# K weights on a second DMA queue, later weights behind the transposes, and a clamp on VectorE: a fused attention and feed-forward kernel

## The chip, the cores and the metric

The kernel runs on one core of one Trainium2 chip. The metric is the device time of one execution in microseconds (us). An execution's time is about 1.7 us more than the span that its profile shows. Medians are quoted with the number of runs. A ratio is the mean time of one kernel's fast runs over that of the other's of the same rounds, so it is not quite the ratio of the medians beside it; its 95% interval stands in brackets. In lines of a profile PE is TensorE, PEld its weight loads, DVE VectorE, ACT ScalarE, POOL GpSimd and SP SyncE; a q behind a name is that engine's instruction queue, L249 a line of kernel.py, and xnT<-xn what an instruction writes and reads.

## The reference

```python
x  = A_x                                   # 1 x 2048 x 576, bf16
xn = layernorm(x)
# A: linear attention, 32 heads of 18
q, k, v = split(xn @ wqkv)                 # 576 x 1728
phi = lambda t: where(t > 0, t + 1, exp(t)) + 1e-6
kv  = sum_s phi(k) v ;  z = sum_s phi(k)
a   = (phi(q) @ kv) / (phi(q) . z + 1e-6) @ wo
# B: gated feed-forward, width 4608
b   = (gelu(xn @ w_gate) * (xn @ w_up)) @ w_down
out = x + a + b
```

## The kernel before: the parts that matter

The order of instructions on each engine is written by hand: every step has a planned time, and the steps are issued sorted by it. Each engine works through its own list in order. A step with a planned time that the chip doesn't keep delays what stands behind it on that engine.

The loads at the start all go through SyncE's queue:

```python
    load_x(0, 1)
    load_x(1, 1)
    load_x(2, 2)
    load_w(1)        # K weights: 576 KB + 72 KB, rows of 1152 bytes
    load_x(4, 2)     # two tiles, rows of 2304 bytes
    load_x(6, 2)
    load_w(0)        # Q weights
    load_x(8, 4)
    load_x(12, 4)
```

For each of 16 tiles of 128 tokens: statistics and norm (VectorE, ScalarE), a transpose (tiles 0 to 3 by TensorE and a copy out of PSUM, tiles 4 to 15 by a crossbar DMA on SyncE's queue), two halves of K (five matmuls each), and the sums G = xn^T phi(K). Twenty Q units run in between and behind. phi is made of four steps per Q unit:

```python
    def q_relu(i): nc.scalar.activation(out=e, in_=ps, func=ACT.Relu, scale=-1.0)        # cut: the tiles
    def q_exp(i):  nc.scalar.activation(out=e, in_=e, func=ACT.Exp, scale=-1.0)
    def q_eps(i):  nc.gpsimd.tensor_scalar(out=e, in0=e, scalar1=1.0, scalar2=EPS_ATT, op0=ALU.mult, op1=ALU.add)
    def q_sum(i):  nc.vector.scalar_tensor_tensor(out=out_, in0=ps, scalar=0.0, in1=e, op0=ALU.max, op1=ALU.add)
```

V's weights and the first gate and up blocks are put between the crossbar transposes, one load each 2.94 us:

```python
    loads = [lambda n, i=i: load_gu(i // 2, i % 2) for i in range(2 * NWBUF)]
    loads.insert(1, lambda n: load_w(2, 0, 2))
    loads.insert(3, lambda n: load_w(2, 2, 4))
    todo += [(18.0 + TILE * i, step, 0) for i, step in enumerate(loads)]
```

Spins (`spin(count)`, matmuls of an identity matrix whose result nobody reads) keep TensorE busy before the first real work.

## Time and profile before

| | before |
|---|---|
| time, median of 4 runs | 525.38 us (524.8 to 525.77) |
| span of the profiled execution (526.45 us, above every timed run) | 524.7 us |
| TensorE busy | 517.2 us, 99% |
| first K matmul; K's main weights landed | 8.24; 8.20 us |
| first gate matmul of the feed-forward | 73.62 us |

TensorE sets the end. Behind 82 us it works without a hole worth naming, so a change to the first part can only move the moment at which the feed-forward starts.

### The profile page before, as it was taken

What the parts mean: (1) busy time and instruction counts of PE and PEld (TensorE: products, weight loads), DVE (VectorE), ACT (ScalarE), POOL (GpSimd) and SP (SyncE); (2) the same over time, 40 slices, a digit from 0 to 9 for tenths busy, and PEclk for the clock granted to TensorE, in tenths of its full rate; (3) what the DMA queues carried; (4) which work ended last, traced back from release to release, by engine and by line L of the source; (5) the groups of instructions that cost most, each with busy time, mean ns of one, the idle gap of its engine ahead of it and who ended that gap; (6) DMA issues with size and microseconds to landing.
All of it is one profiled execution on the core that took longest, in us unless ns stands there. A gap on an engine that the chain in (4) does not pass through costs nothing.

```text
span 524.7 us, 10664 instructions
## 1 busy us (share of the span) xinstructions
PE 517.2 (99%) x4502; PEld 315.8 (60%) x4502; DVE 248.4 (47%) x426; ACT 147.9 (28%) x301; POOL 40.1 (8%) x63
## 2 busy tenths in 40 slices
PE   7999999999999999999999999999999999999997
PEld 7767764555577754444577744444777544445775
DVE  7887545977348423333388134333584233333110
ACT  5989563233230012332200033232000123222000
POOL 2012130121001100000011000000011000000000
PEclk9999999999999999999999999999999999999999
DMA  8565009999500035555300065555100355540000
GB/s 262 135 156 119 1 2 240 264 268 265 169 21 24 12 103 158 158 144 158 108 12 13 28 174 143 156 159 151 32 22 12 104 158 157 144 130 1 12 11 24
DMA packets 106443, 57.90 MB, mean 110 GB/s; under 512 B 13402, under 2 KB 105754, under 8 KB 106394
## 3 DMA queue, kind: packets, MB, share of 16 engines
q1 hardware_dynamic: 106394, 57.21, 38.8%
q8 instruction: 35, 0.57, 0.4%
q14 instruction: 14, 0.11, 0.1%
HBM read 52.86 MB, written 2.36 MB: 105 GB/s over the span
## 4 chain that ended last, share of the span: by engine, by line
PE 96%; DMA 2%; ACT 1%; DVE 0%; SPq 0%; issue 0%; DVEq 0%
PE ps_all L318 55%; PE ps_all L664 27%; PE ps_all L669 4%; PE ps_all L294 3%; PE ps_all L250 3%; PE ps_all L347 3%; DMA wqkv_sb<-in_A_wqkv_dram 1%; DMA xnT<-xn 1%; PE ps_all L442 1%; PE ps_all L424 0%; PE ps_all L646 0%; SPq L93 0%; ACT phi_e L270 0%; DVE hT L278 0%; ACT xnT L239 0%; ACT phi_e L274 0%
## 5 line engine op out<-in xcount | busy, mean ns | idle before, releaser
L318 PE MATMUL ps_all<-xnT,wg 64*128 64x512 bf16 x1152 | 273.0, 376 | 0.0
L318 PE MATMUL ps_all<-xnT,wu 64*128 64x512 bf16 x1152 | 271.6, 376 | 0.0
L635 DVE TENSOR_TENSOR hT<-ps_all,gl 128x512 bf16<-128x512 f32 x144 | 99.4, 691 | 161.2 <-ACT gl L634 160.7
L634 ACT ACTIVATE gl<-ps_all 128x512 f32<-128x512 f32 x144 | 86.0, 598 | 312.7 <-PE ps_all L318 295.8
L318 PEld LDWEIGHTS <-wu 64*128 64x128 bf16 x1152 | 108.1, 94 | 66.0 <-SPq L327 0.7
L318 PEld LDWEIGHTS <-wg 64*128 64x128 bf16 x1152 | 108.1, 94 | 65.7 <-issue 0.5
L664 PE MATMUL ps_all<-wd_sb,hT 128*128 128x288 bf16 x1152 | 147.0, 286 | 0.0
L664 PEld LDWEIGHTS <-hT 128*128 128x128 bf16 x1152 | 112.3, 98 | 30.6 <-issue 1.3
L466 DVE RECIPROCAL den_sb<-den_sb 126x128 f32<-126x128 f32 (+1 forms) x80 | 68.3, 911 | 0.5
L672 DVE TENSOR_TENSOR res<-ps_all,x_sb 128x288 bf16<-128x288 f32 x32 | 14.6, 458 | 88.0 <-PE ps_all L669 88.0
L318 PE MATMUL ps_all<-xnT,wr 64*128 64x512 bf16 x288 | 55.7, 376 | 0.0
L469 POOL TENSOR_TENSOR pqT<-pqT,den_sb 126x512 bf16<-126x512 bf16 (+3 forms) x25 | 24.1, 965 | 299.2 <-DVE den_sb L466 276.0
L669 PE MATMUL ps_all<-m_sb,pqT 126*128 126x288 bf16 (+1 forms) x160 | 24.9, 285 | 0.0
L318 PEld LDWEIGHTS <-wr 64*128 64x128 bf16 x288 | 14.6, 94 | 16.7 <-issue 0.7
L250 PE MATMUL ps_all<-wqkv_sb,xnT 128*128 128x288 bf16 x160 | 22.5, 286 | 1.7 <-DMA wqkv_sb<-in_A_wqkv_dram 0.8
L294 PE MATMUL ps_all<-hT,xn 128*128 128x288 bf16 (+4 forms) x176 | 22.4, 276 | 0.0
L294 PEld LDWEIGHTS <-xn 128*128 128x128 bf16 (+1 forms) x176 | 17.5, 102 | 4.3
L250 PEld LDWEIGHTS <-xnT 128*128 128x128 bf16 x160 | 15.3, 98 | 7.6 <-issue 1.3
L393 DVE SCALAR_TENSOR_TENSOR pqT<-ps_all,phi_e 126x512 bf16<-126x512 f32 (+1 forms) x20 | 13.4, 672 | 12.4 <-POOL phi_e L389 12.4
L669 PEld LDWEIGHTS <-pqT 126*128 126x128 bf16 (+1 forms) x160 | 15.5, 97 | 4.1
L347 PE MATMUL ps_all<-xnT,wqkv_sb 128*126 128x512 bf16 (+1 forms) x70 | 17.4, 378 | 0.0
L389 POOL TENSOR_SCALAR phi_e<-phi_e 126x512 f32<-126x512 f32 (+1 forms) x20 | 12.4, 618 | 54.2 <-DVE hT L278 29.8
(63 smaller groups left out, 183.8 us busy)
## 6 DMA issues: line engine op xcount, KB each, us to landing
wg<-in_B_w_gate_dram SPq DMA_DIRECT2D x72, 256.0 KB, 2.9
wu<-in_B_w_up_dram SPq DMA_DIRECT2D x72, 256.0 KB, 3.5
wd_sb<-in_B_w_down_dram SPq DMA_DIRECT2D x12, 432.0 KB, 4.7
wr<-in_B_w_gate_dram SPq DMA_DIRECT2D x72, 32.0 KB, 2.7
wr<-in_B_w_up_dram SPq DMA_DIRECT2D x72, 32.0 KB, 3.1
out_dram<-res SPq DMA_DIRECT2D x15, 144.0 KB, 1.8
wqkv_sb<-in_A_wqkv_dram SPq DMA_DIRECT2D x2, 576.0 KB, 6.0
x_sb<-in_A_x_dram SPq DMA_DIRECT2D x2, 576.0 KB, 7.2
```

The costliest lines, as they stand in the source:

```text
L250: nc.tensor.matmul(ps_all[:, k_bank(n, hf), :HALF], lhsT=xnT[:, kt, n * P:(n + 1) * P], rhs=wqkv_sb[:, kt, D + hf * HALF:D + (hf + 1) * HALF],
L294: nc.tensor.matmul(ps_all[:m, b, col:col + w], lhsT=xn[:, n, j0:j0 + m], rhs=pk[:, n, d0:d0 + w], start=(n == 0 and col == 0), stop=(n == ...
L318: return nc.tensor.matmul(self.outs[i], lhsT=self.lhs(i, rows, kt), rhs=self.rhs(i, rows, kt), start=start, stop=stop, skip_group_check=True,)
L347: nc.tensor.matmul(ps, lhsT=wqkv_sb[:, kt, q0:q0 + rows], rhs=xnT[:, kt, sc * SC:(sc + 1) * SC], start=(kt == 0), stop=(kt == KT - 1),)
L393: nc.vector.scalar_tensor_tensor(out=out_, in0=ps, scalar=0.0, in1=e, op0=ALU.max, op1=ALU.add)
L466: nc.vector.reciprocal(out=d[:, h:h + P], in_=d[:, h:h + P])
L469: nc.gpsimd.tensor_tensor(out=pqT[:rows, c, cols], in0=pqT[:rows, c, cols], in1=d, op=ALU.mult)
L634: nc.scalar.activation(out=gl[:], in_=ps_all[:, b[0], :], func=ACT.Gelu_apprx_tanh)
L635: nc.vector.tensor_tensor(out=hT[:, GUB * k + i, :], in0=ps_all[:, b[1], :], in1=gl[:], op=ALU.mult)
L664: nc.tensor.matmul(acc, lhsT=hT[:, f, j * P:(j + 1) * P], rhs=wd_sb[:, f, hs], start=(f == 0), stop=False,)
L669: nc.tensor.matmul(acc, lhsT=pqT[:rows, c, ts_], rhs=m_sb[:rows, c, hs], start=False, stop=(c == NCH - 1),)
L672: nc.vector.tensor_tensor(out=res[:, hs], in0=acc, in1=x_sb[:, n, hs], op=ALU.add)
```

## The change

The intent: ScalarE issues the K weights on its own queue, so that they needn't stand behind x tiles in SyncE's; a memset of two elements of the K weights, which the load must wait for, holds it back until the first x tiles are under way. V, gate and up weights no longer mix with the crossbar transposes. The last 8 Q units take exp straight from PSUM and clamp it on VectorE, which spares ScalarE one pass and GpSimd all of its part. A relay (an empty instruction on another engine, which tells TensorE that one half of a block has been written) moves from SyncE to GpSimd for feed-forward block 1. The planned times of nearly all steps change with it. The diff, cut to its core:

```diff
+    def load_w(which, on=nc.sync): ...                       # cut: as before, but in whole, on queue `on`
+    nc.scalar.preload_act_table_set("natural_log_exp_and_others")
     load_x(0, 1)
     load_x(1, 1)
     load_x(2, 2)
-    load_w(1)
-    load_x(4, 2)
-    load_x(6, 2)
+    load_x(4, 4)                                              # rows of 4608 bytes
     load_w(0)
     load_x(8, 4)
     load_x(12, 4)
+
+    nc.vector.memset(wqkv_sb[HP:P, 4, :], 0.0)
+    nc.vector.memset(wqkv_sb[0:1, 0, D:D + 2], 0.0)
+    load_w(1, nc.scalar)
 ...
+    def q_exp1(i): nc.scalar.activation(out=e, in_=ps, func=ACT.Exp)
+    def q_min(i):  nc.vector.tensor_scalar(out=e, in0=e, scalar1=1.0, scalar2=EPS_ATT, op0=ALU.min, op1=ALU.add)
+    def q_max(i):  nc.vector.scalar_tensor_tensor(out=out_, in0=ps, scalar=1.0 + EPS_ATT, in1=e, op0=ALU.add, op1=ALU.max)
 ...                                                           # cut: new planned times of all steps
-    todo += [(t, spin, count) for t, count in [(5.70, 4), (6.23, 3), (6.60, 5), (10.42, 2)]]
+    todo += [(t, spin, count) for t, count in [(5.80, 3), (6.20, 5), (8.50, 2)]]
-    ...                                                       # cut: the loads between the transposes
+    load_w(2)                                                 # behind the last transpose
+    for i in range(NWBUF):
+        load_gu(i, 0)
+        load_gu(i, 1)
-    for step in (q_relu, q_exp, q_eps, q_sum):                # units 12 to 19, three places
+    for step in (q_exp1, q_min, q_max):
-                      nc.sync if blk < 2 else nc.gpsimd)      # relay of a feed-forward block
+                      nc.sync if blk == 0 else nc.gpsimd)
```

## The prediction

> **What bounds the kernel now.** I read the page's busy line and its chain first, to see which engine sets the end.
>
> ```profile
> PE 517.2 (99%) x4502; PEld 315.8 (60%) x4502; DVE 248.4 (47%) x426; ACT 147.9 (28%) x301; POOL 40.1 (8%) x63
> ...
> PE 96%; DMA 2%; ACT 1%; DVE 0%; SPq 0%; issue 0%; DVEq 0%
> ```
>
> TensorE is busy 517.2 of 524.7 us and is 96% of the chain, so only 7.5 us are free at all, and the change removes no real matmul (it drops 4 spin matmuls). The feed-forward part is untouched: three of its four blocks show one unbroken piece of 648 matmuls of 70.03 to 70.04 us in the chain of waits. What can move is the attention head of the program, up to about 82 us. So I listed TensorE's waits in the first 80 us, and then the chain in order of time around each.
>
> ```profile
> PE ps_all L138 <- POOL ident masks.py:199: 1.4, 1, 1.4
> PE ps_all L250 <- DMA wqkv_sb<-in_A_wqkv_dram: 0.8, 1, 0.8
> PE ps_all L250 <- DMA xnT<-xn: 0.7, 1, 0.7
> PE ps_all L236 <- ACT xnT L239: 0.6, 1, 0.6
> PE ps_all L250 <- DVE hT L278: 0.2, 1, 0.2
> ```
>
> ```profile
> 2.20 6.00 DMA wqkv_sb<-in_A_wqkv_dram
> ...
> 8.24 1.40 PE ps_all L250 x10
> ...
> 11.12 0.59 ACT xnT L239
> ...
> 11.75 0.44 PE ps_all L236 x5
> ...
> 15.33 0.83 DVE hT L278 x2
> ...
> 16.20 0.77 PE ps_all L250 x5
> ...
> 25.84 4.52 DMA xnT<-xn
> ...
> 30.41 1.40 PE ps_all L250 x10
> ```
>
> The reader is to see: the first K matmul waits for the K weights, issued at 2.20 and landed 6.00 us later at 8.20. Then there are three holes, before 11.75 (a copy of transposes out of PSUM), 16.20 (a K sum) and 30.41 (a crossbar transpose that took 4.52 us, while others of these transposes took 2.6 to 3.0 us). Together they are 0.6 + 0.2 + 0.7 = 1.5 us. From 30.41 to the feed-forward the chain is TensorE alone.
>
> In the weight-load waits of the stretch 60 to 100 us there is one more, a relay on the sync queue:
>
> ```profile
> PEld L318 <- SPq L327: 0.7, 2, 0.5
> ```
>
> At 80.74 a matmul starts 0.39 us after the one before instead of 0.22, so about 0.2 us of that reaches TensorE.
>
> **What the Trainium skill says.** (1) "DMA: Bandwidth & Descriptors", section "Issuing engines are not separate DMA queues": transfers issued from different engines run on the same 16 DMA engines and interleave; a second issuer saves issue time only. Section "Queues, rings and completion order" of that page adds that each engine round-robins between the queues by packet. The kernel before uses one queue only (page part 3 has all data in q1), so its trace can neither confirm nor deny the sharing. It does show the limit: from 4 to 12 us the DMA share is 0.99 and 1.08 at 313 and 325 GB/s, saturated. (2) "ScalarE: Activation LUTs", section "What ACT_TABLE_LOAD costs": 1283 ns a load; the trace has 1283 ns exactly (0.80 to 2.08 us). (3) "VectorE: DVE Perf Modes", section "The perf-mode tier table (the rule you actually need)": an fp32 tensor_scalar from SBUF runs at 2x, a PSUM operand does not. The trace has no such instruction on VectorE; from PSUM, the 126x512 one takes 0.68 us.
>
> **The change, part by part.**
>
> *K weights on ScalarE's queue.* The issue moves from SyncE at 2.20 us to ScalarE, behind the table load (ends 2.08) and the two memsets on VectorE (the first 0.78 us, from about 0.9: ends near 1.7). So it is issued at about 2.1 to 2.2, no earlier. What changes is the company. Before: first-in first-out behind x tiles 0 to 3 (576 KB), then K (648 KB), and K landed at 8.20. Now x tiles 4 to 7 (576 KB in one transfer with 4608-byte rows instead of two with 2304) are issued on SyncE at about 2.2 and share with K. If K really gets half the engines from about 3.3 us on, with some 350 KB landed by then (117 GB/s over 4 us is 470 KB), it is done when about 350 + 2 x 650 = 1650 KB have moved; at 313 GB/s after 4 us that is about 7.8 us. Larger rows could be quicker per byte: in the kernel before, the two late x transfers of 576 KB landed about 1.4 us apart, against 2.2 us for 576 KB of 1152-byte weight rows. That puts it near 7.3. I take 7.5 for the first K matmul, 0.7 us earlier. Of this 0.3 us goes back, as five transposes (1.40/5 apiece is no guide; 0.28 us between the start of five and what follows at 10.07) now stand behind the first K matmuls instead of ahead of them: net 0.4 us.
>
> *Order of the head.* The instruction orders show K halves, transposes, G sums and Q units reshuffled, with the same work. ScalarE is the tight engine here (3.91 of 4 us busy from 12 to 16, 3.5 to 3.6 to 24). The two holes before 11.75 and 16.20 (0.8 us) are of the old order. I expect new ones in their place, because ScalarE's queue still has copies of transposes between relu and exp: a copy takes 0.69 us, relu 0.41, exp 0.44. Working through the new order by these durations I find three waits of 0.3 to 0.4 us up to the first G sum; but with the second Q unit pulled ahead of the K halves of tile 4, less idle later. Net gain: 0.3 us.
>
> *Later weights behind the transposes.* V and 4 blocks of gate and up weights no longer lie between the 12 transposes. The 4.52 us transpose should be 2.6 to 3.0, and the 0.7 us hole before 30.41 goes. V and the blocks are 18 issues of about 0.45 to 0.6 us, starting near 48: all are issued by about 59 and landed by 62. V is first read at 66.0, block 0 at 73.4. Hidden. Gain: 0.7 us.
>
> *Clamp on VectorE for the last 8 units.* It removes 8 relus (0.60 us, ScalarE) and 8 GpSimd adds (0.62), and adds 8 VectorE min/adds of an estimated 0.33 us (512 elements at 2 per cycle at the page's 0.96 GHz, plus about 60 cycles by the same page). ScalarE's end part, 70.86 to 77.00 before,
>
> ```profile
> 70.86 1.08 ACT L381 ACTIVATE phi_e<-ps_all 126x512 f32<-126x512 f32 x2 [3.64 <-PE ps_all L318]
> ...
> 77.00 1.28 ACT L634 ACT_TABLE_LOAD   x1
> 78.29 1.09 ACT L634 ACTIVATE gl<-ps_all 128x512 f32<-128x512 f32 x2
> ```
>
> shrinks by 6 x about 0.55 = 3.3 us at most; then the first pair of matmul results at about 76.5, not ScalarE, is what the first GELU waits for. But TensorE shows no wait for ScalarE or VectorE there, so of this nothing reaches the end. The relay of feed-forward block 1 moves to GpSimd, which is now idle there: 0.2 us.
>
> Sum: 0.4 + 0.3 + 0.7 + 0.2 = 1.6 us; 525.3 - 1.6 = 523.7 us, which I round down to 523.6 as the two dropped spin groups add a little.
>
> **Rivals.** (a) *K comes no earlier*, or later: if the engines alternate by row and not by bytes, a 4608-byte x row is moved for each 1152-byte K row, and K waits until x tiles 4 to 7 are through, past 8.2 us. For it: the DMA is saturated, and nothing is taken out ahead of K. Against it: K's rows need not queue behind x tiles 2 and 3 any more. Also, x tiles 2 and 3 (landed near 5.4) could come later, and their statistics stand ahead of the copy of tile 0's last transposes on VectorE. Time then about 525. (b) *ScalarE takes over.* From 12 to 48 us it is 85 to 98% busy; a TensorE that starts earlier may just catch it up and wait, so that only part of the gain stays: about 524.5. Against it: TensorE was never seen to wait for it after 12 us. (c) *Everything fits*: K at 7.0, no new holes, 1.2 + 1.5 + 0.2 = 2.9 us: 522.4. (d) *Late weights stall the feed-forward*: would need 11 us of delay; I give it almost nothing.
>
> **Range and chances.** 523.6 us, from 522.3 (rival c) to 525.2 (rival a). Faster by over 2% would need 514.8, more than all 7.5 us of TensorE's idle time; slower by over 2% would need a new stall of 10.5 us, and none is in sight. Within 2%: 0.98.
>
> **What would show it.** First K matmul at 7.3 to 7.8 and K's landing beside it; ScalarE's queue as a second data queue. No transpose above about 3.2 us, and no TensorE wait for one. Table load for GELU near 74 to 75 instead of 77.0. The feed-forward's three unbroken 70.0 us pieces unchanged. TensorE's waits in the first 80 us (without the first, for the identity) down from 2.3 us to about 1. Wrong if K lands after 8.2, if x tiles 2 and 3 land after 6, or if new waits on ScalarE's or VectorE's copies exceed 1.5 us.

## The result, and the profile after

The changed kernel took 526.88 us (median of 4, 526.42 to 527.52) against 525.38: ratio 1.003 [1.0013, 1.0048]. It is about 1.5 us slower, where about 1.7 us less were predicted. It is within 2%, but outside the range and on the wrong side.

The page's busy line and chain of the changed kernel look almost as before:

```profile
PE 517.4 (99%) x4498; PEld 314.8 (60%) x4498; DVE 250.9 (48%) x435; ACT 143.2 (27%) x293; POOL 35.2 (7%) x55
```

"TensorE busy" is no help here: a matmul at half clock counts as busy too. TensorE's waits in the first 80 us, the same view as before (us in total, times, longest):

```profile
PE ps_all L249 <- DMA wqkv_sb<-in_A_wqkv_dram: 3.1, 1, 3.1
PE ps_all L137 <- POOL ident masks.py:199: 1.4, 1, 1.4
PE ps_all L249 <- DMA xnT<-xn: 0.2, 1, 0.2
```

The waits for ScalarE's copy and for VectorE's K sum are gone, as meant, but the wait for K's weights grew from 0.8 to 3.1 us. The chain in order of time (start, duration, what):

```profile
0.80 1.15 ACT L114
1.95 7.64 DMA wqkv_sb<-in_A_wqkv_dram
9.59 0.04 issue
9.63 1.36 PE ps_all L249 x5
10.99 0.53 PE ps_all L235 x5
11.52 1.20 PE ps_all L249 x5
```

K was issued at 1.95, 0.25 us earlier than before, and landed 1.39 us later. The earlier issue won nothing: the first row of K moved at 4.02 us, and at 4.01 in the kernel before. The five K matmuls at 11.52 then took 1.20 us; ten of them took 1.40 us before. Why the rate halved is in the table of stretches (length, busy time of TensorE, its weight loads, VectorE, ScalarE and GpSimd, then the granted TensorE clock, DMA share, GB/s):

```profile
8.00:10.00 2.00, 0.37 (x2) 0.26 (x2) 0.41 (x2) 0.00 (x0) 0.24 (x1) 0.80 1.12 303
10.00:12.00 2.00, 2.00 (x13) 1.45 (x11) 0.00 (x0) 0.85 (x2) 0.00 (x0) 0.50 1.03 315
12.00:14.00 2.00, 2.00 (x20) 1.59 (x18) 1.37 (x4) 1.97 (x7) 0.24 (x1) 0.85 0.69 279
```

After 3.1 us without work the clock was granted at half until some way past 12 us. All four runs have a mean clock of 0.996 or 0.997; the kernel before has 0.999 or 1.000. The Trainium skill ("TensorE: Matmul & The Clock Gate", section "What's actually happening") says that a window of about 3.4 us without work halves the clock and another one of work restores it; the trace agrees in kind: half lasted 3.4 us, from 9.20 to 12.62. But the gap that did it was only 3.1 us long, and in the run b3_no_hold below one of 2.0 us was followed by 3.4 us of half clock as well (9.28 to 12.70), so here less than a whole window without work was enough.

What the DMA engines did, by queue (packets, MB, share of 16 engines; q1 is SyncE's, q10 ScalarE's with nothing but K on it). Between 3 and 4 us, though K had been issued at 1.95, q10 moved nothing:

```profile
q1 hardware_dynamic: 86, 0.16, 97.2%
```

Between 4 and 6 us:

```profile
q1 hardware_dynamic: 171, 0.58, 73.8%
q10 hardware_dynamic: 174, 0.20, 29.5%
```

And between 7 and 8 us, when x tiles 4 to 7 were nearly through and the Q weights followed them:

```profile
q10 hardware_dynamic: 177, 0.20, 55.4%
q1 hardware_dynamic: 163, 0.19, 53.4%
```

In these two stretches the queues moved about as many packets each (nearly all of them rows): 174 of K to 171 of the other. But most x rows of the first stretch were 4608 bytes long and a K row 1152, so K got 0.20 of 0.78 MB. When the Q rows came, as short as K's, K got half and no more, and from 8 to 9 us only 97 of 292 packets. Before, all of this stood behind K in one queue. That the engines take turns row for row is no rule, though: two runs below (a2_x_small_rows, b5_only_k_queue) gave K clearly more than half of the rows.

Later in the chain, the slow crossbar transpose that the change was to remove:

```profile
45.96 4.34 DMA xnT<-xn
50.35 1.40 PE ps_all L249 x10
```

No weight load is beside it any more (the first is issued at 50.22), and still it took 4.34 us. ScalarE's end part, as shown of before:

```profile
72.47 1.09 ACT L398 ACTIVATE phi_e<-ps_all 126x512 f32<-126x512 f32 x2 [4.31 <-PE ps_all L317]
74.41 2.05 ACT L398 ACTIVATE phi_e<-ps_all 126x512 f32<-126x512 f32 x4 [0.86 <-issue]
76.47 1.28 ACT L647 ACT_TABLE_LOAD   x1
78.25 0.60 ACT L647 ACTIVATE gl<-ps_all 128x512 f32<-128x512 f32 x1 [0.49 <-PE ps_all L317]
```

ScalarE now waits for TensorE ahead of the first GELU (0.49 us) rather than the other way round.

### The profile page after: what moved, and what is told of

Its sections match the earlier page's. It is cut to its first block, busy times and chain, and to the rows that moved or that the text cites. A ratio compares the mean times of both kernels' runs of the same rounds, so it can differ in the third digit from the quotient of the medians.

```text
span 525.2 us, 10640 instructions
## 1 busy us (share of the span) xinstructions
PE 517.4 (99%) x4498; PEld 314.8 (60%) x4498; DVE 250.9 (48%) x435; ACT 143.2 (27%) x293; POOL 35.2 (7%) x55
## 4 chain that ended last, share of the span: by engine, by line
PE 97%; DMA 2%; ACT 0%; DVE 0%; issue 0%
PE ps_all L317 55%; PE ps_all L677 27%; PE ps_all L249 4%; PE ps_all L682 4%; PE ps_all L293 4%; PE ps_all L346 2%; DMA wqkv_sb<-in_A_wqkv_dram 1%; DMA xnT<-xn 1%; PE ps_all L455 1%; PE ps_all L437 0%; PE ps_all L659 0%; ACT L114 0%; PE ps_all L235 0%; DVE res L685 0%; ACT phi_e L269 0%; PE ps_all L426 0%
## 5 line engine op out<-in xcount | busy, mean ns | idle before, releaser
L249 PE MATMUL ps_all<-wqkv_sb,xnT 128*128 128x288 bf16 x160 | 23.6, 296 | 3.3 <-DMA wqkv_sb<-in_A_wqkv_dram 3.1
L277 DVE SCALAR_TENSOR_TENSOR hT<-ps_all,phi_e 128x288 bf16<-128x288 f32 x32 | 13.2, 449 | 8.1 <-ACT phi_e L273 7.5
L269 ACT ACTIVATE phi_e<-ps_all 128x288 f32<-128x288 f32 x32 | 12.9, 410 | 6.8 <-PE ps_all L249 5.5
```

The source lines that it names most:

```text
L249: nc.tensor.matmul(ps_all[:, k_bank(n, hf), :HALF], lhsT=xnT[:, kt, n * P:(n + 1) * P], rhs=wqkv_sb[:, kt, D + hf * HALF:D + (hf + 1) * HALF],
```

## The experiments

Twelve kernels ran, in three calls of four; kernels of one call ran on the same chip and share the runs of the kernel before. All gave correct results. The table is the summary; "K landed" is the main part of the K weights in the profiled execution.

| run | K landed | first K matmul | clock | median (runs) | ratio to before |
|---|---|---|---|---|---|
| before, profiled / changed | 8.20 / 9.59 | 8.24 / 9.63 | 1.000 / 0.996 | 525.38 / 526.88 (4) | 1.003 [1.0013, 1.0048] |
| a1_k_sync | 7.94 | 7.99 | 1.0 | 523.71 (4) | 0.9979 [0.9964, 0.9994] |
| a2_x_small_rows | 8.30 | 8.34 | 0.999 | 525.71 (4) | 1.0019 [1.0002, 1.0036] |
| a3_warm | 9.31 | 9.36 | 1.0 | 526.36 (4) | 1.0035 [1.0011, 1.0059] |
| a4_clamp_only | 7.59 | 7.63 | 1.0 | 524.80 (4) | 0.9996 [0.9982, 1.0011] |
| b1_after_again | 10.44 | 10.48 | 0.997 | 527.47 (5) | 1.0038 [1.0025, 1.0051] |
| b2_warm_full | 10.14 | 10.18 | 1.0 | 526.69 (5) | 1.0029 [1.0017, 1.0041] |
| b3_no_hold | 5.64 | 8.60 | 0.997 | 525.57 (6) | 1.0008 [0.9996, 1.002] |
| b5_only_k_queue | 8.65 | 8.69 | 1.0 | 526.56 (5) | 1.0028 [1.0016, 1.004] |
| c3_no_hold_reordered | 5.42 | 6.82 | 0.997 | 525.64 (5) | 1.001 [0.9998, 1.0023] |
| b4_only_late_loads | 7.59 | 7.63 | 1.0 | 524.94 (5) | 0.9998 [0.9985, 1.0011] |
| c4_k_sync_fetch_moved | 7.08 | 7.12 | 1.0 | 524.77 (5) | 0.9991 [0.9979, 1.0004] |
| c1_k_before_x2 | 7.34 | 7.38 | 1.0 | 524.49 (5) | 0.9984 [0.997, 0.9997] |

My theory: the private queue made K late, because the engines share by rows; the gap cooled the clock; the rest of the change is harmless or good. The rivals: the new order is itself slow; the engines share by bytes and K is late only because there is too much in flight; the slow clock is hidden behind the other engines.

**K back on SyncE's queue.** The changed kernel with:

```diff
     load_x(2, 2)
+    load_w(1)
     load_x(4, 4)
...
-    nc.vector.memset(wqkv_sb[0:1, 0, D:D + 2], 0.0)
-    load_w(1, nc.scalar)
```

> The changed kernel with the K weights back on SyncE's queue, between x tiles 2-3 and x tiles 4-7, and without the two-element memset that held them back; all else as changed. Theory (the lateness of K is the queue's doing: on its own queue K alternates with the 4608-byte x rows and then with the Q rows): K lands near 8.2 us instead of 9.59, TensorE's hole ahead of the first K matmul is 1.5 us or less and its clock stays 1.0, the whole takes about 523.5 to 524.5 us. Rival (the new order of the head, or the loads moved behind the transposes, costs the time): K lands near 8.2 but the time stays at 526 or more.

K landed at 7.94 us and the time fell to 523.71 us, 0.2% under the kernel before. TensorE's waits now:

```profile
PE ps_all L136 <- POOL ident masks.py:199: 1.4, 1, 1.4
PE ps_all L248 <- DMA wqkv_sb<-in_A_wqkv_dram: 0.9, 1, 0.9
PE ps_all L248 <- DMA xnT<-xn: 0.7, 2, 0.4
```

So the queue of K is the whole loss; with K on SyncE's queue the other parts together cost nothing (0.9979 here; 0.9991 [0.9979, 1.0004] in c4_k_sync_fetch_moved, the same with 12 more spins). The rival that blamed the new order falls.

**Short x rows.** Is it the row length? The changed kernel with:

```diff
-    load_x(4, 4)
+    for n in range(4, 8):
+        load_x(n, 1)
```

> The changed kernel with x tiles 4 to 7 loaded by four transfers with rows of 1152 bytes in place of one with rows of 4608 bytes; K stays on ScalarE's queue. Theory (the 16 DMA engines take turns by row, so K's 1152-byte rows lose to 4608-byte ones): K gets half of the bytes instead of under a third from 3.5 us on and lands at 7.8 to 8.6 us; time about 524.5. Rival (they share by bytes, K is late only because the total is too much): K lands at 9.4 to 9.8 as before, time 526 to 527.

K landed at 8.30 us, in the expected range. The same two lines for 4 to 6 us:

```profile
q10 hardware_dynamic: 362, 0.42, 64.6%
q1 hardware_dynamic: 189, 0.24, 35.5%
```

With the same K on the same queue, K got 0.42 of 0.66 MB instead of 0.20 of 0.78, so an even split by bytes is refuted. But 362 packets to 189 isn't an even split by rows either. SyncE here also issued more slowly (four transfers for one, and the Q weights later), which may be a part of why K got more than half; and with the row length the number and size of the transfers changed too, so this run doesn't part the two. The time came down only to 525.71: in two of the four runs the mean clock was 0.997 or 0.996, as after a stretch of half clock; their traces weren't kept, so what made it isn't shown. I had expected 524.5; short rows mend the profiled run, not all runs.

**A warm clock.** What did the half clock cost? The changed kernel with 45, and later 55, more spins in the hole:

```diff
-    [(5.80, 3), (6.20, 5), (8.50, 2)]
+    [(5.80, 3), (6.20, 50), (8.50, 2)]        # second run: 60
```

> The changed kernel with 45 more spin matmuls in the hole ahead of the first K matmul. Theory (the 3.1 us without work lets TensorE's clock drop to half for about 3.4 us, and that slow stretch costs time at the end): granted clock stays 1.0 from 9 to 13 us, ten K matmuls take 1.3 us instead of 2.5, and the time falls by 0.7 to 1.4 us to about 525.5 to 526.2. Rival (the slow stretch is hidden, as ScalarE is behind anyway): same time within 0.3 us.

> The changed kernel with 55 more spins, so that the hole ahead of the first K matmul is nearly filled (45 left 0.5 us of it). Theory (the slow clock after the hole costs time at the end): 0.6 to 1.2 us faster than the changed kernel of the same call. Rival (the slow stretch is hidden, ScalarE and VectorE are behind anyway): within 0.3 us of it.

The clock stayed at 1.0 in both profiled runs:

```profile
8.00:10.00 2.00, 1.68 (x31) 1.56 (x28) 0.69 (x3) 0.00 (x0) 0.24 (x1) 1.00 1.11 337
10.00:12.00 2.00, 1.82 (x17) 1.40 (x17) 0.00 (x0) 0.92 (x3) 0.00 (x0) 1.00 1.08 320
```

(the second one, stretches as above). In the first, the times alone decide little: 526.36, with one run of 528.65 (whose mean clock was 0.997, spins or not). The second ran beside the changed kernel itself (next paragraph): 526.69 against 527.47, 0.8 us less, though the two ratios' intervals overlap. In the traces, from the first K matmul to the first gate matmul took 65.84 us with the cold clock and 64.48 with the warm one. Of these 1.4 us, 0.4 come with a slow transpose that the cold run had and the warm one not; the other 0.9 us are there before it. The same comparison of the changed kernel's trace with a3_warm's gives 0.5 us before the slow transpose. So the clock cost 0.5 to 0.9 us.

**The changed kernel once more**:

> The changed kernel once more, beside the three others on one chip, so that they can be compared with it directly. All theories: 1.0 to 2.2 us slower than the kernel before (525.2 to 525.6); K lands at 9.2 to 9.8 us.

527.47 us, ratio 1.0038. K landed at 10.44 us, outside the 9.2 to 9.8 that I expected. On the private queue K landed between 9.31 and 10.44 in four profiled executions of this head (spins added or not), and on SyncE's queue with x tiles 0 to 3 ahead between 7.08 and 8.20 in five. The means, 9.87 and 7.68, differ by 2.2 us.

**K's queue alone**, in the old order:

```diff
-    load_w(1)                                  # between load_x(2, 2) and load_x(4, 2)
...
+    nc.vector.memset(wqkv_sb[0:1, 0, D:D + 2], 0.0)
+    load_w(1, on=nc.scalar)                    # behind the other loads; table load put first
```

> The kernel before with nothing changed but the K weights on ScalarE's queue, held back by the memset, in the old order of the head; x tiles 4 to 7 still come as two transfers with rows of 2304 bytes. Theory (this part alone makes the loss): K lands at 8.6 to 9.6 us and the time is 0.8 to 2.5 us above the kernel before. Rival (the loss is the new order's): time within 0.4 us of the kernel before.

526.56 us, 1.4 us more than the kernel before. K landed at 8.65, the small part of it (the last 64 rows) only at 9.73. Here x tiles 4 to 7 have rows of 2304 bytes. Between 4 and 6 us:

```profile
q10 hardware_dynamic: 270, 0.31, 52.4%
q1 hardware_dynamic: 163, 0.33, 47.3%
```

K got more of the bytes than beside rows of 4608 (0.31 of 0.64 MB) and came earlier, which is the direction that the row theory wants. But turns row for row would have given it as many rows as the other queue, not 270 to 163. What the engines' turns go by stays open; what is shown is that K's part was smallest beside the one large transfer with 4608-byte rows. This one part of the change makes the loss that the whole change shows.

**Without the hold.** K issued at 0.84 us, beside x tiles 0 and 1:

```diff
-    nc.vector.memset(wqkv_sb[0:1, 0, D:D + 2], 0.0)
```

> The changed kernel without the two-element memset, so that ScalarE issues K at about 0.9 us, beside the first x tiles. Theory (rows alternate between the queues): against 1152-byte rows of x tiles 0 and 1 K gets half, K lands at 7.0 to 8.2 us, x tile 0 lands 0.3 to 0.8 us later (3.3 to 3.9); TensorE's clock stays 1.0 and the time is 1 to 3 us less than the changed kernel, about 523.5 to 525. Rival (the hold is needed: the first x come so late that the first K matmul is no earlier): time as changed or more.

K landed at 5.64 us, much earlier than I expected, but x tile 1 only at 6.25. Its statistics stand ahead of the norm of tile 0 on VectorE, and TensorE waited 2.0 us for that:

```profile
1.26 4.99 DMA x_sb<-in_A_x_dram
...
6.27 0.83 DVE stats L210 x2
```

Between 3 and 4 us the queues didn't alternate at all:

```profile
q10 hardware_dynamic: 282, 0.32, 93.9%
q1 hardware_dynamic: 35, 0.03, 8.5%
```

x tile 1 had been issued at 1.26, 0.42 us behind K, and moved almost nothing while K ran. It is the changed kernel's stretch from 3 to 4 us the other way round: in both, what was issued first moved first, whichever queue it was on. Why is open. The time is 525.57, 0.4 us above the kernel before and 1.9 below the changed one of the same call: the hold costs more than it protects.

**Without the hold, reordered.** Statistics, rstd and norm of tile 1 behind the copy of tile 0, and those of tiles 2 and 3 later:

```diff
-        (ln_stats, [3.15, 4.09, 5.57, 7.12, ...
-        (ln_rstd, [4.27, 5.21, 6.69, 8.82, ...
+        (ln_stats, [3.15, 6.60, 6.90, 7.12, ...
+        (ln_rstd, [4.27, 6.70, 8.60, 8.82, ...   # cut: norm and dup likewise
```

> The changed kernel without the hold, and with the statistics of x tile 1 moved behind the norm and copy of tile 0 on VectorE (with the hold gone, tile 1 landed at 6.25 us and blocked them, while K was there at 5.64). Theory (the late first K matmul of the version without the hold was VectorE's order, not K): the first K matmul starts at 7.0 to 7.6 us, TensorE's clock stays at 1.0, time 523 to 524.5. Rival (K beside the first x is a loss whatever the order): time above 525.

The first K matmul started at 6.82 us, earlier than in any other run, and the time was no better: 525.64. The wait moved on to the norms:

```profile
PE ps_all L234 <- DVE xn L219: 3.5, 3, 1.5
```

Three waits of up to 1.5 us for tiles 0 to 2 took its place. VectorE's order was the reason for the first wait, as my theory said, but x tiles 2 and 3 landed at 6.99 us (5.56 in the changed kernel), and the gain is gone. The profiled run, the slowest of the five, also had half clock from 11.19 to 14.60. This expectation's time was a miss.

**K ahead of x tiles 2 and 3**, on SyncE's queue:

```diff
-    load_x(2, 2)
     load_w(1)
+    load_x(2, 2)        # statistics and norm of tiles 2 and 3 behind the norm of tile 1
```

> A version that may beat both kernels: as the variant with K on SyncE's queue, but K is issued ahead of x tiles 2-3, and the statistics of tiles 2 and 3 stand behind the norm of tile 1. Theory (the first K matmul waits for bytes ahead of K in the queue): K lands at 6.6 to 7.3 us, the first K matmul starts at 7.0 to 7.4, x tiles 2-3 land at 7.6 to 8.3; 0.3 to 1.3 us less than with K behind them, 522.5 to 523.5. Rival (what is won at the first K matmul is lost waiting for tile 2): time 523.5 to 524.5.

The first K matmul started at 7.38, and TensorE then waited 1.5 us for tile 2 (a wait for "ACT rstd"). 524.49 us, ratio 0.9984: better than the kernel before, but not better than with K behind these tiles. The rival had 523.5 to 524.5, and it was right.

**The clamp alone**, put into the kernel before:

> The kernel before with only the clamp of the last 8 Q units moved to VectorE. All theories: ScalarE reaches the GELU table load 2 to 3 us earlier, TensorE has no wait there to lose, so 525.4 within 0.4 us of the kernel before. If the clamp costs, it is over 525.8.

524.80 us, ratio 0.9996: nothing that times can show. The GELU table load started 1.2 us behind the first gate matmul (73.69 and 72.46) instead of 3.4 us (77.00 and 73.62).

**Late loads alone**, put into the kernel before:

> The kernel before with nothing changed but the V, gate and up loads put behind the 12 crossbar transposes. Theory (a slow transpose comes of a 16 KB fetch of TensorE's instructions that falls into its data phase, 1.6 to 2.1 us after its issue, not of the weight loads beside it): at least one transpose still takes over 4 us if a fetch falls so, and the time is within 0.4 us of the kernel before. Rival (the weight loads made the transpose slow, as the prediction had it): none takes over 3.2 us, and the time is about 0.7 us less.

524.94 us, ratio 0.9998. No gain, where I had predicted 0.7 us. In this profiled run no transpose took over 3.5 us, so it doesn't say by itself what makes one slow.

**What makes a transpose slow.** Between 45 and 51 us of the changed kernel, nothing but transposes, the beginning of V's load and one more packet were on the DMA engines:

```profile
q8 instruction: 1, 0.02, 1.3%
```

It is a fetch of 16 KB of instructions, which held one DMA engine for 1.23 us from 47.89. With 45 more spins (90 more TensorE instructions) these fetches came earlier, at 12.16, 23.79 and 41.43 instead of 15.02, 31.25 and 47.89, so they are TensorE's. In the 12 traces of the experiments and the 2 of before and changed there are 14 x 12 = 168 transposes. Nine took over 4 us, and each of them had such a fetch begin 1.6 to 2.2 us after its issue:

| run | transpose issued, took | fetch began | behind the issue by |
|---|---|---|---|
| before | 25.84, 4.52 | 27.83 | 1.99 |
| changed | 45.96, 4.34 | 47.89 | 1.93 |
| a1_k_sync | 13.54, 4.37; 43.80, 4.43 | 15.16; 45.87 | 1.62; 2.07 |
| a4_clamp_only | 43.21, 4.30 | 45.27 | 2.06 |
| b1_after_again | 46.98, 4.41 | 48.91 | 1.93 |
| b3_no_hold | 45.20, 4.72 | 47.25 | 2.05 |
| c4_k_sync_fetch_moved | 24.72, 4.25; 43.32, 4.21 | 26.92; 45.53 | 2.20; 2.21 |

A fetch 0.4 to 1.1 us behind the issue went with 2.9 to 3.5 us; one 2.3 us or more behind with 2.6. At 2.2 us some were slow and some not. Smaller fetches fit too: three transposes with an 8 KB instruction fetch (on queue q14) 2.1 us behind their issue took 3.4 to 3.8 us, and no transpose of the 168 took over 3.2 us without a fetch of either kind that began at its issue or up to 2.2 us behind it. I tried to move the fetches away, with 12 more spins in the version with K on SyncE's queue:

> The variant with K on SyncE's queue (its transposes at 13.54 and 43.8 us took 4.4 us), plus 12 spins in an idle stretch of TensorE before the first K matmul, so that the instruction fetches of TensorE come 1.3 to 1.8 us earlier in its program. Theory (instruction fetch): the fetch near 45.9 comes near 44.3, under 1 us after the issue of the transpose at 43.8, and no transpose there takes over 3.6 us; the wait of TensorE near 48.3 (0.6 us) is gone, time about 0.3 to 0.6 us less, 523.2. Rival (slow transposes come of something else): the one near 43.8 is slow again.

The first two fetches moved by 1.9 and 2.3 us, but the one near 45.9 only to 45.53, and as the whole run was earlier too, it fell onto a transpose again, as did the second. Two transposes were slow, both with a fetch. The time, 524.77, is no gain over the version without these spins. As a test by moving this failed; the coincidence in nine of nine is strong, but it was observed and not made.

## Why the prediction was wrong

**The step that failed** is the first, in the prediction's words "If K really gets half the engines from about 3.3 us on" and "I take 7.5 for the first K matmul, 0.7 us earlier". It was 9.63, 1.4 us later. K's first row moved at 4.02 us and not at 3.3, and then it did not get half: between 4 and 6 us it had 0.20 of 0.78 MB. The total was not the error: the sum's 1650 KB had moved by about 7.2 us, sooner than the 7.8 it gave, but only 0.41 of K's 0.66 MB were among them. The Q weights, which I had not put into the sum at all, took half of the rest and more. I had quoted the skill that the engines take turns by packet, and then counted bytes.

**Rival (a)** had what happened in this kernel right, "a 4608-byte x row is moved for each 1152-byte K row", and the size wrong: "about 525". It counted a later K and not what a hole of 3.1 us does to the clock (0.5 to 0.9 us), nor the Q rows. Its last fear, x tiles 2 and 3 landing late, did not come: 5.56 us against 5.40.

**"Order of the head", 0.3 us**, is not shown. With K on SyncE's queue the rest of the change gave 1.1 us (a1_k_sync, 0.9979) or, in the same kernel with 12 more spins, 0.5 us (0.9991). The clamp and the late loads alone gave none of it that could be measured. But about 0.8 us of it lies at the other end of the kernel: from the end of TensorE's last matmul to the end of the span 3.73 us passed before, and 2.96 and 2.97 in these two (why, is the last point of the last section). From the first K matmul to the first gate matmul they took 65.2 and 65.4 us; in the old order it was 65.4 before, and 64.8 and 64.5 in a4_clamp_only and b4_only_late_loads. The two holes of the old order were gone in the changed kernel's waits, but no trace shows that the new order is faster up to the feed-forward, and I didn't run it alone.

Reading the planned times for this I found something that no run tested: in both kernels the K sum of tile 1's first half is planned (13.41 and 16.55 us) behind the first G sum (12.97 and 11.96), which starts the same PSUM bank 0 anew. By the program that sum reads G and not K for this half tile, and the trace of before agrees: the K sum at 15.33 us waited 0.38 us for a G matmul (L294). All runs passed the comparison with the reference nevertheless; whoever takes this kernel further should put the sum first.

**"Later weights behind the transposes", 0.7 us**, failed. The measured gain is 0.02% with an interval of 0.13% to either side, and the slow transpose moved from 25.84 to 45.96 us instead of going away. I had read the loads beside it as its cause, with no more to go on than that they were there. That the loads themselves stay hidden was right: the last gate and up block had landed by 63.4 us, and the first gate matmul came at 75.23.

**The clamp** was right in that TensorE gained nothing measurable, and too hopeful about ScalarE: it did reach its table load earlier, but by 2.1 us rather than 3.3, counted from the first gate matmul. **The relay, 0.2 us**: the changed kernel's trace has no weight-load wait from 60 to 100 us any more, where the one before had 0.7 us.

**Range and chances**: within 2% was right; the upper end, 525.2, was set by a rival whose mechanism was right and whose size was wrong. Three slips in the text moved nothing: one group of spins was dropped (14 spins became 10), not two; rival (b) read ScalarE as 85 to 98% busy from 12 to 48 us, but from 28 to 32 it was 74% (2.95 of 4 us); and rival (c) comes to 522.4, not 522.3.

The profiled executions understate the loss: their spans are 524.7 and 525.2 us, because the one of before was that kernel's slowest. Up to the first gate matmul the changed one lost 1.61 us. Of this 0.4 us was back by the end of TensorE's last matmul (521.01 and 522.19), and 0.8 us more came back at the very end (see the last section).

## What to carry to other kernels

A second DMA queue isn't a bypass. It shares the same engines, and beside one large transfer with long rows K got a quarter of the bytes (0.20 of 0.78 MB): what must land first belongs early in one queue, with nothing big issued beside it. If a wait ahead of TensorE's first real work may come near 2 to 3 us, keep it spinning: holes of 2.0, 3.1 and 3.4 us were each followed by 3.4 us of half clock here. Holes of up to 1.6 us were not, but for one run (c3_no_hold_reordered) in which three of 0.8, 1.5 and 1.3 us came close together. And before a slow transfer is put down to its neighbours, look in the trace for what shares its engine at that moment, instruction fetches too.

## What the Trainium skill lacked or had wrong

- "DMA: Bandwidth & Descriptors", section "Queues, rings and completion order": it says that an engine drains a packet of about 9 to 17 descriptors before it turns to another queue. What is lacking is what share two queues get. In 2 us K's queue moved 174 packets (0.20 MB) to 171 (0.58 MB) beside mostly 4608-byte rows, 270 (0.31) to 163 (0.33) beside 2304-byte rows and 362 (0.42) to 189 (0.24) beside mostly 1152-byte rows: an even split neither of rows nor of bytes fits all three.
- The same section: nothing on two queues not sharing at all. Issued 0.42 us behind a K transfer on the other queue, an x tile moved 35 packets to 282 of K in 1 us; issued 0.22 us behind an x transfer, K moved none to 86 in 1 us.
- "Runtime: NRT & Kernel Launch", section "Instruction fetch mechanics", lacks this: a crossbar transpose took 4.2 to 4.7 instead of 2.6 us in nine cases, each with a 16 KB instruction fetch that began 1.6 to 2.2 us after its issue.
- "VectorE: DVE Perf Modes", section "The TRN2 errata": with the 58 cycles of its table I estimated 0.33 us for the 126x512 fp32 clamp; it took 0.42 us. With the fixed term of about 150 cycles, which the same section gives as measured, the estimate comes to (150 + 256) / 0.96 GHz = 0.42 us, and that term is the one to use here.
- No page that I read has this: ScalarE's DMA issue doesn't wait for its table load. K was issued at 1.95 us, and at 0.84 in b3_no_hold, while the load ran from 0.80 to 2.08.
- No page that I read has this: the end of a kernel depends on which semaphore its last store has. SyncE waits for all DMA semaphores in a fixed order at the end. In the kernel before, the last store was issued at 521.54 of a span of 524.7 us, 3.2 us before the end; in the changed one at 522.71 of 525.2, 2.4 us before. The store itself took 1.6 us in both. The trace's waits show its semaphore in the first of six waits before, with the others behind it, and in the sixth after. In all 14 traces the two go together: nine with it in the sixth wait ended 2.96 to 2.98 us behind TensorE's last matmul, five with it in the first or second 3.29 to 3.73 us. No run changed this alone.
